# Moving 183 tasks of an ordered five-engine program to other places in their engine's order

## The chip, the cores and the metric

The kernel runs on one core of a Trainium2 chip. The core has five engines with an instruction queue each: TensorE (PE in the profile), ScalarE (ACT), VectorE (DVE), GpSimd (POOL) and SyncE (SP, which here only issues transfers), and 16 DMA engines that move the data. The metric is the device time of one execution in microseconds (us). Before the change it is 190.21 us, the median of three runs (189.45 to 190.45).

## The reference

A gated linear attention is followed by a feed-forward block. Only the order of operations matters here:

```python
f = 1.0 / (1.0 + np.exp(-f_logit))               # B, H, S, D = 4, 8, 768, 48
for t in range(S):
    state = f[:, :, t, :, None] * state + np.einsum('bhd,bhe->bhde', k[:, :, t], v[:, :, t])
    y[:, :, t] = np.einsum('bhd,bhde->bhe', q[:, :, t], state)
x = y.transpose(0, 2, 1, 3).reshape(B * S, H * D)   # 3072 x 384
h = x @ w_in                                     # 384 x 2048
g = h * (1.0 / (1.0 + np.exp(-h)))
out = g @ w_out                                  # 2048 x 384
```

## The kernel before

The sequence of 768 steps is cut into 6 chunks of 128, and there are 4 batches: 24 units, numbered u = 0 to 23, four units of one chunk after the other. Two neighbouring units form a pair P. Each unit is a chain of small tasks, and each task belongs to one engine. In the names below the number is the unit (or its pair's first unit), and for the feed-forward tasks a second number is the piece.

- SP: `f`, `k`, `q`, `v` load a unit (192 KB each) or, from unit 4 on, a pair (384 KB each), all at L485. `wi_0..3` (L505) and `wo_0..3` (L510) load the weights, 768 KB each. `qkD` and `xD` transpose by DMA for later units (L592, L625), `so` (L562) stores a unit's output; units up to 10 are stored from POOL, the others from SP.
- ACT: `E`, `L` (L492, L494) make the logarithm of the gate; `ia`, `a`, `al` (L572, L574, L576) are exponentials of its running sum; `s1` and `si` (L526, L536) are the SiLU of a feed-forward piece. SiLU and the exponentials need different function tables, so a table load (L680) stands wherever the order goes from one kind to the other. `co_2` is a weight cast.
- PE: `cs` (L565, L569) the running sum; `tq` (L588) a transpose of q and k; `sc` (L599) the scores; `y` (L608, L612) the chunk's output; `yT` (L620) its transpose; `d` (L630) the state's increment; `m1` (L529, one unit) and `mi` (L540, a pair) the first feed-forward product in pieces; `mo` (L551) the second one, four tasks a unit.
- DVE: `qg` (L582), `qkc` (L590), `at` (L603), `yc` (L616), `xc` (L622), `sd` (L635, L637), the output copies `oa` and `oc` (L554, L559), and the casts `ci_3`, `co_1`.
- POOL: `ki` (L578), `vb` (L580), `su` (L641, the new state), the early stores, and the casts `ci_0`, `ci_1`, `ci_2`, `co_0`, `co_3` (L520).

The chain of one unit is `f, E, L, cs, ia, a`; then `qg` (needs `a` and `q`) and `ki` (needs `ia` and `k`); then `tq` and `qkc` (or `qkD`), `sc`, `at`, `y`, `yc`, `yT` and `xc` (or `xD`). Then `m1`/`mi` of piece j (needs the x of its units and the weight cast `ci`), `s1`/`si`, `mo`, `oc`, `so`.

The order is decided while the program is built, not on the chip. `make_tasks` (L81) lists the tasks with dependencies, buffers and priorities. `schedule` (L208) plays them through an estimate, first free, which yields one fixed order per engine, and then once more with that order; this second pass hands out the buffer numbers. `planned` (L376) joins the two. `idle` (L386) finds stretches in which PE is expected to wait, and fills them with multiplications of a block of zeros (`warm`, L650, matmuls at L653). Then each task is emitted, and each engine works off its tasks strictly in this order.

Many buffers are few: one PSUM bank each for `cs`, `tq`, `sc` and `yd` (used by `y` and `d`), three for the feed-forward products (`mlp`), two staging buffers `wt` for the four `wo` pieces, three output buffers `o`. So a task also waits until the earlier user of its buffer has been read. For instance `cs_5` needs the only `cs` bank, which `qg_4` still reads; and `wo_2` needs the staging buffer that `co_0` empties.

```python
    schedule(tasks, slots, cfg, cfg["margin"])
    fixed = {e: sorted([t for t in tasks if t.eng == e], key=lambda t: (t.start, t.idx)) for e in ENGINES}
    schedule(tasks, slots, cfg, 0.0, fixed=fixed)
```

Of the kernel before, what the change touches and what calls it, by code (L numbers as in the profile page):

```python
# [24 lines left out]
    margin=0.35,  # L25
# [11 lines left out]
    first=0,  # L37
# [25 lines left out]
ROW = {2: 0.097, 4: 0.178, 6: 0.235}  # L63
CAST_ENGINES = ('DVE', 'ACT', 'POOL')
CAST = dict(DVE=0.9, ACT=1.3, POOL=1.6)
DMA = dict(f=LOAD, k=LOAD, q=LOAD, v=LOAD, qkD=TURN, xD=TURN, wi=WEIGHT, wo=WEIGHT, so=STORE)


class Task:
    def __init__(self, name, eng, dur, prio, deps=(), acq=(), use=(), mode=None, phase=None, load=0.0):  # L70
        self.name, self.eng, self.dur, self.prio = name, eng, dur, prio
        self.deps, self.acq, self.use = list(deps), list(acq), list(use)
        self.mode, self.phase, self.load = mode, phase, load

# [6 lines left out]
def make_tasks(cfg):  # L81
# [4 lines left out]
    def add(name, *a, **k):  # L86
        t = Task(name, *a, **k)
        T[name] = t
        tasks.append(t)
        return t  # L90
# [78 lines left out]
    for j in range(4):  # L169
        for m, (x, w, N) in enumerate((("wi", "ws", NI), ("wo", "wt", NO))):  # L170
            e = cfg["cast"][4 * m + j]
            add(("ci" if x == "wi" else "co", j), e, CAST[e], cfg["rank0"]["cw"] + 1.0 * j + 4.0 * m, deps=[T[x, j * N // 4]], use=[I[w, j * N // 4]])

# [31 lines left out]
    return tasks, T  # L205


def schedule(tasks, slots, cfg, margin=0.0, fixed=None, dur=None):  # L208

    for i, t in enumerate(tasks):  # L210
        t.idx, t.start, t.end, t.succ, t.ready, t.left = i, None, None, [], 0.0, len(t.deps)
# [17 lines left out]
    q = {"hw": [], "sw": []}  # L229
    events, pend = [0.0], []  # L230
    events.append(busy["SP"])
    now, dma_t, done, EPS = 0.0, 0.0, 0, 1e-7

    def finish(t, when):
        nonlocal done
        t.end = when
        done += 1
        lat = LAT[t.eng] if not t.load else 0.06
        for s in t.succ:
            l = (0.15 if s.eng == "ACT" else 0.0) if s.eng == t.eng and not t.load else lat  # L240
            if s.eng == "PE" and t.eng != "PE":
                l += margin
            s.ready = max(s.ready, when + l)
            s.left -= 1
            if not s.left:
                waiting[s.eng].append(s)
            heapq.heappush(events, s.ready)
        for x in dict.fromkeys([*t.acq, *t.use]):
            x.users -= 1
            if not x.users:  # L250
                free[x.cls].append((when + lat, x.slot))
                heapq.heappush(events, when + lat)

    def heads():
        h = q["hw"][0] if q["hw"] and q["hw"][0][2] <= dma_t + EPS else None
        s = q["sw"][0] if q["sw"] and q["sw"][0][2] <= dma_t + EPS else None
        if h and s:
            rate = (h[4] / (h[4] + s[4]), s[4] / (h[4] + s[4]) * 1.04)
        else:
            rate = (1.0, 1.0)  # L260
        nxt = [x[0][2] for x in q.values() if x and x[0][2] > dma_t + EPS]
        if h:
            nxt.append(dma_t + h[1] / rate[0])
            over = sum(x[1] for x in q["hw"]) - DEPTH
            if over > EPS:
                nxt.append(dma_t + over / rate[0] + EPS)
        if s:
            nxt.append(dma_t + s[1] / rate[1])
        return h, s, rate, min(nxt) if nxt else None

    def dma_to(upto):
        nonlocal dma_t
        while dma_t < upto - EPS:
            h, s, rate, nxt = heads()
            step = min(upto, nxt if nxt is not None else upto) - dma_t
            dma_t += step
            for k, v, r in (("hw", h, rate[0]), ("sw", s, rate[1])):
                if v:
                    v[1] -= r * step
                    if v[1] <= EPS:  # L280
                        q[k].pop(0)
                        if q[k] and q[k][0][4] != v[4] and k == "hw" and TURN[2] in (q[k][0][4], v[4]):
                            q[k][0][1] += cfg["turn_cost"]
                        heapq.heappush(pend, (dma_t + v[3], v[0].idx))
                        heapq.heappush(events, dma_t + v[3])

    def can(t):
        need = {}
        for x in t.acq:
            if x.slot is None:  # L290
                need[x.cls] = need.get(x.cls, 0) + 1
        return all(sum(f <= now + EPS for f, _ in free[c]) >= n for c, n in need.items())

    def pick(e, cand):
        key = lambda t: (t.prio, t.idx)
        if e != "ACT":
            return min(cand, key=key)
        best = {m: min((t for t in cand if t.mode == m), key=key, default=None) for m in ("exp", "silu")}
        free_one = min((t for t in cand if t.mode is None), key=key, default=None)
        mine, other = best[st["mode"]], best["silu" if st["mode"] == "exp" else "exp"]  # L300
        if free_one and (mine is None or free_one.prio < mine.prio):
            return free_one
        if other is None:
            return mine
        if mine is None:
            oldest = min(max(t.ready, st["last"]) for t in cand)
            hold = cfg["hold_" + st["mode"]]
            if now + EPS >= oldest + hold:
                return other
            heapq.heappush(events, oldest + hold)  # L310
            return None
        return other if other.prio < mine.prio - cfg["keep_" + st["mode"]] else mine

    n = 0
    while done < len(tasks):
        n += 1
        if n > 100000:
            raise RuntimeError("no end")
        while events and events[0] <= now + EPS:
            heapq.heappop(events)  # L320
        dma_to(now)
        while pend and pend[0][0] <= now + EPS:
            when, i = heapq.heappop(pend)
            finish(tasks[i], when)
        moved = True
        while moved:
            moved = False
            for e in engines:
                if busy[e] > now + EPS or (e == "SP" and sum(x[1] for x in q["hw"]) > DEPTH + 2 * EPS):
                    continue  # L330
                if fixed is not None:
                    if at[e] == len(fixed[e]):
                        continue
                    t = fixed[e][at[e]]
                    if t.left or t.ready > now + EPS or not can(t):
                        continue
                    at[e] += 1
                else:
                    cand = [t for t in waiting[e] if t.ready <= now + EPS and can(t)]
                    t = pick(e, cand) if cand else None  # L340
                    if t is None:
                        continue
                    waiting[e].remove(t)
                moved = True
                begin = now
                if t.mode is not None and t.mode != st["mode"]:
                    st["mode"] = t.mode
                    begin = max(begin, st["last"] + TABLE)
                for x in t.acq:
                    if x.slot is None:  # L350
                        got = min(fs for fs in free[x.cls] if fs[0] <= now + EPS)
                        free[x.cls].remove(got)
                        x.slot = got[1]
                t.start = begin
                busy[e] = begin + D(t)
                if e == "ACT":
                    st["last"] = busy[e]
                heapq.heappush(events, busy[e])
                if t.load:
                    sp = e == "SP"  # L360
                    first, land, packet = DMA[t.name[0]]
                    q["hw" if sp else "sw"].append([t, t.load, now + first, land, packet])
                else:
                    heapq.heappush(pend, (busy[e], t.idx))
        nxt = heads()[3]
        nxt = [x for x in (events[0] if events else None, pend[0][0] if pend else None, nxt) if x is not None]
        if not nxt:
            raise RuntimeError(f"stuck at {now:.2f}: {[t.name for t in tasks if t.end is None][:12]}")
        now = max(min(nxt), now + 1e-5)
# [6 lines left out]
def planned(cfg, slots):  # L376

    tasks, T = make_tasks(cfg)
    schedule(tasks, slots, cfg, cfg["margin"])
    fixed = {e: sorted([t for t in tasks if t.eng == e], key=lambda t: (t.start, t.idx)) for e in ENGINES}  # L380
    schedule(tasks, slots, cfg, 0.0, fixed=fixed)
    order = sorted(tasks, key=lambda t: (t.start, t.idx))
    return order, idle(order, slots, cfg)

# [326 lines left out]
```

## Time and profile before

| quantity | value |
|---|---|
| time, median of 3 runs | 190.21 us (189.45 to 190.45) |
| the profiled execution's own time | 188.87 us |
| its span, first to last instruction | 187.1 us |
| PE busy | 174.3 us (93% of the span) |
| ACT busy | 131.1 us (70%) |
| DVE busy | 95.8 us (51%) |
| POOL busy | 70.6 us (38%) |
| read from and written to HBM | 25.17 MB, 4.72 MB |
| granted PE clock | 1.00 |

The profile comes from one execution; its own time is 1.77 us longer than its span. Busy time of PE contains the filling matmuls on zeros (10.6 us) and the overlap of pipelined matmuls, so that it is not a measure of useful work. For that the start times of neighbouring tasks on PE are of more use: the distance from one task's first matmul to the next one's. An entry such as `atm L603 <- PE sc L599` in the waits means that the DVE instruction at L603, which writes `atm`, waited for the matmuls at L599. In the chain of work an entry of SPq is the time in which SP issues a transfer, and an entry of DMA is a transfer in flight.

### The profile page before, as it was taken

The page shows a single profiled execution, that of the slowest core. Times are in us where ns is not written, and L with a number is a line of the kernel's source. Part 1 is how long each engine was busy: PE and PEld are TensorE (multiplying, and loading weights), DVE is VectorE, ACT ScalarE, POOL GpSimd, SP SyncE. Part 2 cuts the span into 40 slices and gives each one's busy share as a digit, 9 for nine tenths or more (in the row PEclk, how much of TensorE's full clock was granted, in tenths as well). Part 3 has the DMA queues.
Part 4 walks back from the last instruction along what each step waited for, and adds up shares of the span by engine and source line. Part 5 has one row for each costly group of instructions (what it writes and reads, how often), then busy time and mean ns, then how long its engine had stood idle before and what let it go on. Part 6 is the DMA issues. An engine that isn't in the chain of part 4 may idle for free.

```text
span 187.1 us, 4715 instructions
## 1 busy us (share of the span) xinstructions
PE 174.3 (93%) x1925; PEld 134.0 (72%) x1925; DVE 95.8 (51%) x185; ACT 131.1 (70%) x217; POOL 70.6 (38%) x112
## 2 busy tenths in 40 slices
PE   5987768989999999979999999999999999999991
PEld 2454758667878879768787786678688886966960
DVE  4269436425877773565527736875542415261011
ACT  4442845988797898998988788668669996810810
POOL 2337647345727470561752742490352006000000
PEclk9999999999999999999999999999999999999999
DMA  6999999999989999999597589588996566413101
GB/s 125 217 216 333 381 351 303 277 191 251 244 193 224 223 246 237 217 226 217 126 185 169 129 177 179 101 118 209 186 151 169 129 121 135 103 21 105 46 17 67
DMA packets 120389, 34.22 MB, mean 183 GB/s; under 512 B 116128, under 2 KB 117792, under 8 KB 120368
## 3 DMA queue, kind: packets, MB, share of 16 engines
q1 hardware_dynamic: 119664, 31.76, 78.3%
q0 software_dynamic: 704, 2.16, 3.2%
q8 instruction: 15, 0.25, 0.5%
q14 instruction: 6, 0.05, 0.1%
HBM read 25.17 MB, written 4.72 MB: 160 GB/s over the span
## 4 chain that ended last, share of the span: by engine, by line
PE 70%; SPq 11%; DMA 8%; ACT 5%; issue 2%; POOL 1%; DVE 1%; DVEq 0%; ACTq 0%
PE mlp L551 29%; PE mlp L540 24%; DMA q<-in_q_dram 8%; SPq L485 7%; PE mlp L529 4%; PE sc L599 3%; SPq L505 3%; PE yd L612 2%; PE yd L608 2%; PE cs L565 2%; ACT L680 2%; PE tq L588 1%; PE yd L630 1%; SPq L510 1%; ACT hT L536 1%
## 5 line engine op out<-in xcount | busy, mean ns | idle before, releaser
L551 PE MATMUL mlp<-w_out,hT 128*128 128x384 bf16 x384 | 69.9, 326 | 0.0
L536 ACT ACTIVATE hT<-mlp 128x512 bf16<-128x512 f32 x72 | 41.7, 597 | 17.4 <-PE mlp L540 14.9
L540 PE MATMUL mlp<-xT,w_in 128*128 128x256 bf16 x432 | 51.5, 273 | 1.1 <-ACT hT L536 1.0
L551 PEld LDWEIGHTS <-hT 128*128 128x128 bf16 x384 | 34.8, 97 | 19.5
L540 PEld LDWEIGHTS <-w_in 128*128 128x128 bf16 x432 | 46.3, 114 | 3.2 <-issue 1.3
L578 POOL TENSOR_TENSOR qk<-k,ia 128x384 bf16<-128x384 f32 x24 | 24.0, 1000 | 53.2 <-ACT al L576 33.2
L603 DVE TENSOR_TENSOR atm<-sc,triu 128x512 bf16<-128x512 f32 x48 | 30.9, 685 | 19.6 <-PE sc L599 19.6
L680 ACT ACT_TABLE_LOAD x23 | 29.5, 1283 | 0.4
L641 POOL TENSOR_TENSOR st<-sd,al 48x192 bf16<-48x192 f32 x40 | 21.0, 524 | 15.8 <-DVE sd L635 8.6
L572 ACT ACTIVATE ia<-cs 128x384 f32<-128x384 f32 x24 | 11.8, 490 | 15.4 <-PE cs L569 10.4
L616 DVE CAST yb<-yd 128x384 bf16<-128x384 f32 x24 | 13.3, 554 | 15.9 <-PE yd L612 15.8
L559 DVE COPY o<-mlp 128x384 f32<-128x384 f32 x22 | 12.2, 556 | 17.8 <-PE mlp L551 14.1
L529 PE MATMUL mlp<-xT,w_in 128*128 128x128 bf16 x288 | 18.7, 220 | 1.9 <-DVE w_in L520 1.6
L582 DVE TENSOR_TENSOR qk<-q,cs 128x384 bf16<-128x384 f32 x24 | 13.2, 550 | 13.4 <-ACT cs L574 8.4
L529 PEld LDWEIGHTS <-w_in 128*128 128x128 bf16 x288 | 16.9, 114 | 2.7 <-DVE w_in L520 1.8
L526 ACT ACTIVATE hT<-mlp 128x512 bf16<-128x512 f32 x24 | 13.6, 597 | 6.8 <-PE mlp L529 6.4
L580 POOL CAST vb<-v 128x384 bf16<-128x384 f32 x24 | 11.6, 505 | 8.9 <-DMA v<-in_v_dram 8.8
L492 ACT ACTIVATE e<-f 128x768 f32<-128x768 f32 (+1 forms) x14 | 10.5, 747 | 5.9 <-DMA f<-in_f_logit_dram 5.9
L635 DVE TENSOR_TENSOR sd<-yd,st 128x384 f32<-128x384 f32 x16 | 8.9, 555 | 8.3 <-PE yd L630 6.2
L574 ACT ACTIVATE cs<-cs 128x384 f32<-128x384 f32 x24 | 11.4, 477 | 0.6
L653 PE MATMUL mlp<-blank 128*128 128x512 bf16 (+3 forms) x32 | 10.6, 466 | 1.0 <-DVE blank L660 1.0
L494 ACT ACTIVATE lf<-e 128x768 bf16<-128x768 f32 (+1 forms) x14 | 10.5, 750 | 0.3
(43 smaller groups left out, 143.9 us busy)
## 6 DMA issues: line engine op xcount, KB each, us to landing
f<-in_f_logit_dram SPq DMA_DIRECT2D x10, 384.0 KB, 5.7
k<-in_k_dram SPq DMA_DIRECT2D x10, 384.0 KB, 5.9
q<-in_q_dram SPq DMA_DIRECT2D x10, 384.0 KB, 5.9
v<-in_v_dram SPq DMA_DIRECT2D x10, 384.0 KB, 5.6
ws<-in_moe_w_in_dram SPq DMA_DIRECT2D x4, 768.0 KB, 9.0
wt<-in_moe_w_out_dram SPq DMA_DIRECT2D x4, 768.0 KB, 8.0
out_dram<-o SPq DMA_DIRECT2D x13, 192.0 KB, 2.1
out_dram<-o POOLq DMA_DIRECT2D x11, 192.0 KB, 3.9
```

What stands on the lines that cost most here:

```text
L485: nc.sync.dma_start(out=dst, in_=SRC[x].rearrange("b h s d -> s (b h) d")[c * C:(c + 1) * C, b * H:(b + n) * H])
L526: return nc.scalar.activation(at("hT", P)[:, 4 * j:4 * j + 4, i * C:(i + 1) * C], h, AF.Silu)
L529: nc.tensor.matmul(h[:, r, :], w_tile(kk, 4 * j + r), at("xT", P)[:, kk, i * C:(i + 1) * C], start=(kk == 0), stop=(kk == KT - 1))
L536: return nc.scalar.activation(at("hT", P)[:, 2 * j:2 * j + 2, :], h, AF.Silu)
L540: nc.tensor.matmul(h[:, i, :], w_tile(kk, n), at("xT", P)[:, kk, :], start=(kk == 0), stop=(kk == KT - 1))
L551: nc.tensor.matmul(o, at("hT", P)[:, n, i * C:(i + 1) * C], w_rows(n), start=(n % (NT // 2 if half else NT) == 0), stop=(n == NT - 1 or ha ...
L578: nc.gpsimd.tensor_mul(at("qk", u)[:, 1, :, 0:D], at("k", P)[:, i], at("ia", u))
L582: nc.vector.tensor_mul(at("qk", u)[:, 0, :, 0:D], at("q", P)[:, i], at("cs", u)[:, 0:HD].rearrange("p (h d) -> p h d", d=D))
L603: nc.vector.tensor_mul(at("atm", u)[:, r], at("sc", u)[:, r], triu[:, None, :].to_broadcast([C, NP, C]))
L616: nc.vector.tensor_copy(at("yb", u), at("y", u))
L641: nc.gpsimd.tensor_mul(at("st", u)[lo:lo + D, :, r * D:(r + 1) * D], at("sd", u)[lo:lo + D, :, r * D:(r + 1) * D], at("al", u)[lo:lo + D, ...
L680: nc.scalar.preload_act_table_set(SETS[after[t.idx]])
```

## The change

The fixed orders are made as before. Then 183 named tasks are taken out of their engine's list (63 of PE, 36 of ACT, 35 of POOL, 26 of DVE, 23 of SP), and each is put back right behind another named task of the same engine. The second pass runs with these lists. It also uses longer estimates for the weight transfers and casts, and counts every landing 0.3 later. That pass fixes three things: the order across engines in which tasks are emitted, which buffer number each task gets, and where and how many zero matmuls fill PE (158 units of 128 columns instead of 112). No task is added or removed.

```diff
 CAST = dict(DVE=0.9, ACT=1.3, POOL=1.6)
+SECOND, LATE, CAST_DUR = dict(wi=2.09, wo=1.95), 0.3, dict(DVE=1.12, ACT=1.3, POOL=1.47)
 DMA = dict(f=LOAD, k=LOAD, q=LOAD, v=LOAD, qkD=TURN, xD=TURN, wi=WEIGHT, wo=WEIGHT, so=STORE)
+MOVED = (
+    ("cs_1", "y_0"), ("tq_1", "d_0"), ("sc_1", "tq_1"), ("yT_1", "sc_2"), ("m1_0_1", "m1_1_1"),
+    ("m1_0_2", "m1_1_2"), ("m1_0_3", "yT_2"), ("m1_1_0", "m1_2_1"), ("sc_3", "m1_2_0"), ("m1_2_2", "m1_2_3"),
...
+    ("yT_8", "y_9"), ("cs_10", "yT_8"), ("mo_6_1", "d_8"), ("mi_4_1", "mi_4_2"), ("mi_4_0", "sc_10"),
+    ("tq_11", "cs_12"), ("d_9", "tq_11"), ("mi_4_4", "mi_4_5"), ("mi_4_3", "mi_4_4"), ("sc_11", "mi_4_6"),
...
+    ("yT_12", "cs_15"), ("yT_13", "cs_16"),
+    ("mi_6_0", "mi_6_1"), ("cs_17", "mi_6_2"), ("mi_6_3", "mi_6_4"), ("mi_6_5", "mi_6_6"), ("y_14", "mo_11_0"),
...
+    ("sc_22", "mi_10_2"), ("mo_21_0", "mo_20_1"), ("mo_21_3", "mi_11_0"), ("al_0", "E_1"), ("E_2", "al_0"),
+    ("L_2", "L_1"), ("al_1", "a_1"), ("E_3", "al_1"), ("al_2", "a_2"), ("ia_3", "al_3"), ("s1_1_3", "s1_2_1"),
...
+    ("si_3_1", "si_3_2"), ("si_3_0", "si_3_1"), ("E_14", "E_12"), ("si_4_5", "si_4_2"), ("L_14", "E_16"),
...
+    ("ci_3", "xc_2"), ("qg_3", "sd_2"), ("xc_3", "yc_3"), ("oa_0", "xc_3"), ("sd_4", "qg_6"), ("qg_7", "xc_5"),
...
+    ("oc_12", "sd_15"), ("xc_14", "qg_19"), ("qg_20", "yc_18"), ("sd_17", "qg_21"), ("oc_14", "sd_17"),
+    ("sd_18", "oc_15"), ("sd_19", "oc_16"), ("ci_1", "ki_1"), ("vb_2", "ci_2"), ("su_0", "ki_3"), ("co_3", "vb_3"),
+    ("su_2", "co_3"), ("so_2", "vb_5"), ("su_3", "so_2"), ("so_3", "ki_6"), ("vb_7", "ki_7"), ("su_4", "vb_7"),
...
+    ("su_6", "ki_10"), ("so_5", "su_8"), ("so_4", "ki_11"), ("so_6", "so_4"), ("su_9", "vb_14"), ("ki_12", "so_7"),
+    ("vb_13", "ki_13"), ("vb_15", "su_10"), ("ki_14", "vb_15"), ("su_11", "vb_17"), ("so_8", "su_11"),
+    ("ki_16", "su_13"), ("su_12", "ki_16"), ("vb_18", "su_14"), ("su_15", "su_16"), ("vb_20", "ki_21"),
+    ("vb_21", "su_17"), ("su_19", "ki_22"), ("vb_23", "ki_23"), ("f_2", "v_0"), ("wi_1", "q_1"), ("f_3", "k_2"),
+    ("v_3", "f_4"), ("wo_3", "v_3"), ("k_6", "q_6"), ("v_6", "f_8"), ("q_8", "v_8"), ("f_10", "v_10"),
+    ("k_10", "f_10"), ("f_12", "v_12"), ("q_16", "f_14"), ("k_14", "q_14"), ("q_12", "f_16"), ("v_14", "q_12"),
...
+)
@@
+        self.label = "_".join(str(x[0] if isinstance(x, tuple) else x) for x in name)
@@
-                    q["hw" if sp else "sw"].append([t, t.load, now + first, land, packet])
+                    q["hw" if sp else "sw"].append([t, t.load, now + first, land + late, packet])
@@
-    schedule(tasks, slots, cfg, 0.0, fixed=fixed)
+    by = {t.label: t for t in tasks}
+    for name, _ in MOVED:
+        fixed[by[name].eng].remove(by[name])
+    for name, after in MOVED:
+        line = fixed[by[name].eng]
+        line.insert(line.index(by[after]) + 1 if after else 0, by[name])
+    for t in tasks:
+        t.load = SECOND.get(t.name[0], t.load)
+        t.dur = CAST_DUR[t.eng] if t.name[0] in ("ci", "co") else t.dur
+    schedule(tasks, slots, cfg, 0.0, fixed=fixed, late=LATE)
```

The orders that result, where the prediction speaks of them (before, then after):

```
SP   before  f_0 k_0 q_0 v_0 f_1 k_1 q_1 v_1 f_2 k_2 q_2 v_2 wi_1 f_3 wi_2 wo_1 wi_3 k_3 wi_0 q_3 wo_0 wo_3 v_3 f_4 wo_2 k_4 q_4
SP   after   f_0 k_0 q_0 v_0 f_2 f_1 k_1 q_1 wi_1 v_1 k_2 f_3 q_2 v_2 wi_2 wo_1 wi_3 k_3 wi_0 q_3 wo_0 f_4 v_3 wo_3 wo_2 k_4 q_4
POOL before  ki_0 vb_0 ki_1 vb_1 su_0 ki_2 vb_2 ci_1 ci_2 su_1 ki_3 ci_0 su_2 co_0 co_3 vb_3 su_3 ki_4
POOL after   ki_0 vb_0 ki_1 ci_1 vb_1 ki_2 ci_2 vb_2 su_1 ki_3 su_0 ci_0 co_0 vb_3 co_3 su_2 ki_4
PE   before  m1_1_3 d_2 m1_2_1 tq_3 m1_0_0 m1_1_0 sc_3 m1_2_0 m1_2_2 m1_2_3 mo_0_0 mo_0_1 y_3 mo_1_0 mo_1_1 d_3 yT_3 mo_2_0 mo_2_1 cs_4 m1_3_0 m1_3_1 mo_2_2 mo_2_3 cs_5 tq_4
PE   after   m1_1_3 d_2 m1_2_1 m1_1_0 tq_3 m1_0_0 m1_2_0 sc_3 m1_2_3 m1_2_2 mo_0_0 y_3 mo_0_1 yT_3 mo_1_0 d_3 mo_1_1 mo_2_0 cs_4 mo_2_1 m1_3_0 m1_3_1 mo_2_2 mo_2_3 cs_5 tq_4
ACT  both    s1_2_0 s1_2_2 s1_2_3 E_4 L_4 co_2 ia_4 al_4 a_4
ACT  before  si_3_7 ia_10 al_10 a_10 E_12 L_12 ia_11 al_11 a_11 E_14 si_4_0
ACT  after   si_3_7 ia_10 al_10 a_10 E_12 E_14 L_12 ia_11 al_11 a_11 si_4_0
```

## The prediction, made before the run

> **What bounds the kernel now.** I first read the head of the page and its slices of time (tenths busy, 4.7 us each).
>
> ```profile
> span 187.1 us, 4715 instructions
> PE 174.3 (93%) x1925; PEld 134.0 (72%) x1925; DVE 95.8 (51%) x185; ACT 131.1 (70%) x217; POOL 70.6 (38%) x112
> ...
> PE   5987768989999999979999999999999999999991
> ...
> DMA  6999999999989999999597589588996566413101
> ```
>
> PE is full after some 30 us; before that it has holes, and the DMA engines are full instead. Then the waits of PE alone:
>
> ```profile
> PE cs L565 <- ACT lf L494: 2.2, 2, 1.1
> PE mlp L529 <- DVE w_in L520: 1.6, 1, 1.6
> PE mlp L540 <- ACT hT L536: 1.0, 1, 1.0
> ...
> PE tq L588 <- DVE qk L582: 0.8, 1, 0.8
> PE cs L565 <- DVE qk L582: 0.8, 1, 0.8
> ```
>
> That is little, but fillers hide waits. So I gathered the instruction list by task and took start-to-start distances on PE. They hardly scatter: `m1` 0.67, `mi` 0.655, `mo` 0.65, `tq` 0.44, `sc` 0.33, `y` 0.37 (0.20 in the first chunk), `d` and `yT` 0.17, `cs` 0.265 (0.16 in the last chunk). Times their counts these make 158.9 us. `cs_0` starts at 4.56 and the last task ends at 183.1, so 19.6 us are lost between tasks: 14.5 before `tq_3` starts at 28.77, 0.92 at `cs_5` (41.31), 1.14 at `mi_4_3` (82.48), 0.23 at `mi_6_3` (109.26), and some 0.1 ahead of each `sc`. The work is not changed; the losses are all there is to win, and from 28.8 on about 2.3 us of them are waits.
>
> What holds the two larger ones? The chain of work, by start and length, ahead of `cs_5`:
>
> ```profile
> 30.42 1.48 POOL w_out L520
> 31.89 0.02 issue
> 31.91 0.53 SPq L510
> 32.44 0.04 issue
> 32.48 0.43 SPq L485
> 32.92 0.04 issue
> 32.96 7.62 DMA q<-in_q_dram
> ```
>
> SP stands still from 27.20 until POOL's `co_0` has emptied the staging buffer that `wo_2` needs; behind `wo_2` come `k_4` and `q_4`. `q_4` lands at 40.58, `qg_4` ends at 41.26 and frees the `cs` bank. At 82 us it is ACT (start, length):
>
> ```profile
> 74.85 1.28 ACT L680 ACT_TABLE_LOAD   x1
> 76.15 0.49 ACT L572 ACTIVATE ia<-cs 128x384 f32<-128x384 f32 x1
> ...
> 79.70 0.84 ACT L492 ACTIVATE e<-f 128x768 f32<-128x768 f32 x1
> 80.54 1.28 ACT L680 ACT_TABLE_LOAD   x1
> ```
>
> Two table loads and 4.38 us of exponentials lie between `si_3_7` and `si_4_0`, and only three `mlp` banks cover them.
>
> **What the skill says.** The Trainium skill, "PSUM — Partial Sum Buffer", section "Engine vs sequencer instructions", has ScalarE, VectorE and GpSimdE queues as strict FIFO and matmuls in program order; the trace agrees (SP, too, holds `k_4` for 4.7 us behind `wo_2`). "DMA: Bandwidth & Descriptors", "Specifications", asks for 512 B and more for line rate: here 192 B rows moved at about 0.22 MB per us and the weights' 2 KB and 6 KB rows at about 0.4. Its section "Issuing engines are not separate DMA queues" says that transfers share the same engines whoever issues them. So early stores on POOL compete with loads. "ScalarE: Activation LUTs", "What ACT_TABLE_LOAD costs", gives 1.28 us and a drain of 1.38 for each switch; the trace shows 1283 ns and an idle gap of 1.31 in all, no drain. I use 1.31.
>
> **The change part by part.**
>
> *Up to 28 us.* `wi_1` goes ahead of `v_1, k_2, q_2, v_2`, `f_2` ahead of `f_1`, `cs_1` behind `y_0`. By landing distances (single load 0.87, first weight 3.75, later weights 2.0) `wi_1` lands near 13.7 instead of 17.5, `f_3` near 16.1 instead of 18.25, `k_2` and `q_2` some 4 us later. `E_3` now stands before `ia_2` on ACT, so unit 2 starts late: `ia_2` 16.7 instead of 13.8. Yet `sc_2` comes at about 19.7 as before, and `m1` starts at 20.7 instead of 20.06. All this has cover: before, PE stood 1.85 us at `m1_0_3` for `ci_3`, whose weight lands at 24.40. `ci_3` now waits for `xc_2` too, about 0.2 later, but `yT_2` is done before it. Had `f_3` no more than a us of further delay, nothing follows.
>
> *The anchor at 28.* `wi_0`, `q_3` and `wo_0` have the same transfers ahead of them in both orders, on full DMA engines: 27.30, 28.07 and 29.95 as before. `ci_0` runs behind `su_0` (ends about 27.4) until 28.9, and `m1_1_0`, now ahead of `tq_3`, starts at 28.95. In tasks of the lengths above, PE reaches the point behind `sc_3` and the three `m1` 0.15 later than before.
>
> *To `cs_5`.* PE now does `m1_2_3` before `m1_2_2`, but ACT keeps `s1_2_2` before `s1_2_3`: `s1_2_3` ends at 34.5 instead of 33.84, then table 1.31, `E_4`, `L_4` end at 37.5 (36.87). PE comes to `cs_4` at 37.0: a new wait of 0.55. From there 3.6 us of tasks lead to `cs_5` at 41.1. The other limit: `su_2` leaves the way of `co_0`, which runs from the landing of `wo_0`, 29.95, to 31.45 instead of 31.89; `wo_2` and `q_4` come 0.4 earlier, 40.2, and `cs_5` could start at 40.9. The later limit holds: 41.1, **0.2 won**.
>
> *41 to 67.* Swaps of `m1`/`mo` pieces, `E_6` before `a_5` (`tq_5` 0.25 later, inside its slack), `cs_9` 3 us later (its reader `ia_9` waits for a table load anyway), late stores `so_0, so_1, so_4`. I compared each place with the end of its producers and bank: no PE task loses more than 0.05. **0.**
>
> *67 to 84.* `cs_10` and `yT_8` go behind `mi_3_7` (0.435 together): `mi_3_7`, `si_3_7` and the table load come 0.46 earlier. ACT then does the same 4.38 us; it ends on `a_11`, so that one step is a little longer, 4.5. `si_4_0` ends at 82.1, and PE resumes at 82.15 with the same tasks done: **0.35 won**. Cover needed: `f_14` must land before 77.5; it moves from 76.92 to about 75.1.
>
> *Afterwards.* `ki_12` waits behind `so_7` (2.5 later), `ki_16` behind `so_8, so_9, so_10, su_13` (2.7 later); `qkD_12` and `qkD_16`, with `v_18` and `f_20` behind them on SP, follow. `sc_12` had 3.74 and `sc_16` 3.55 of slack, `E_20` 2.92: just covered, and lost one for one beyond that. At `mi_6_3` the pieces follow ACT's order: 0.15 of 0.23 won. `oc_14` behind `sd_17` makes `mi_8_1` 0.05 late. The end (copy, store, 4 us) stays.
>
> *Fillers* add 46 units, 56 ns each when warm, 2.6 us, in waits for `ci_3`, `ci_0` and the first units: nothing while those waits last.
>
> Sum: 0.2 + 0.35 + 0.15 - 0.05 = 0.65 us. The profiled execution of 188.87 becomes 188.2; the median of 190.21, which is 1.34 above it, becomes **189.55**.
>
> **Rivals.**
>
> *Early weight, early gain.* The first weight piece took 3.75 us between landings, the later ones 2.1: a start loss of 1.65. If small loads around `wi_1` fill it, `wi_0`, `ci_0`, `wo_0` and `q_4` all come about 1.6 earlier, and PE keeps it through `cs_5`: 190.21 - 0.65 - 1.6 = 188.0. For it: DMA moved less than usual at 13 to 15 us. Against: `f_3` was queued there already and did not fill it.
>
> *The start loss paid twice* (the slower side). After `wi_1` come five small loads, then `wi_2`. If a weight behind small loads always starts so slowly, `wi_0` lands at 28.95, and `ci_0`, PE and `cs_5` are 1.65 late: 190.21 - 0.65 + 1.65 = 191.2. It decides from 0.65 on, and makes 0.5% from 1.6. For it: `wi_1` itself. Against: `wi_0` and `wo_0`, each behind one small load, took 2.1 and 1.9.
>
> *Nothing.* New waits like the one at `cs_4` may eat all: 190.2. Half of the moves change the order of pieces that are never late.
>
> **How the numbers follow.** Chances: forecast 45% (189.0 to 190.1), early gain 25% (187.4 to 188.7), paid twice 22% (190.7 to 191.8), nothing 8%. 0.5%, 0.95 us, is about what a measurement of this kernel can tell from no change, so the border is 189.26 and 191.16. The forecast lies at it: a third of it, all of the early gain: 0.40 faster. Two thirds of the paid-twice case and a remainder of unseen stalls: 0.20 slower. The rest, 0.40, within. The range leaves out the outer parts of both rivals: 187.9 to 191.4.
>
> **What would show it.** SP's issue of `wo_2` near 31.5; `wi_0` landing near 27.3 (26 or 29 for the rivals); a wait of `cs_4` for `L_4` of about half a us near 37; `cs_5` near 41.1; the PE wait for `hT` near 82 at 0.6 instead of 1.0; no wait at `sc_12`, `sc_16`. A wait of PE over 0.3 us anywhere after 84 us, or a landing of `wi_0` more than 0.7 from 27.3, makes the prediction wrong.

## The result and the profile after

The changed kernel is slower: 190.9 us, the median of 22 runs, beside 189.88 us, the median of 22 runs of the kernel before. The ratio is 1.0053, with a 95% interval from 1.0031 to 1.0074, so about 1.0 us (0.6 to 1.4) was lost where 0.65 was to be won. Ratios and their intervals, here and below, leave out the few executions over 1.5% slower than the fastest of their kernel, and are worked out from all the others, not from the two medians printed beside them. The three runs known before had their median at 190.21; the 22 have it 0.33 lower. The profiled execution of the changed kernel took 191.54 us, 0.6 more than its median, and the one of before, 188.87, is below its own; the pair of profiles therefore shows a larger difference (2.7 us of span) than the medians, and single times read from it below carry some of that scatter.

The head of the page and its slices, after the change:

```profile
span 189.8 us, 4733 instructions
...
PE 177.3 (93%) x1938; PEld 134.2 (71%) x1938; DVE 95.8 (50%) x185; ACT 129.4 (68%) x217; POOL 70.3 (37%) x112
...
PE   5988778998999999999999999998999999999991
...
DMA  6998999999998999989979549969898805611201
```

The span is 2.7 us longer. PE is 3.0 us busier; the zero matmuls account for it, as their busy time rose from 10.6 to 13.8 (46 more units, some 70 ns each by this, where the prediction had 56). The waits of PE (sum, count, longest):

```profile
PE yd L663 <- POOL vb L631: 1.6, 1, 1.6
PE cs L616 <- ACT lf L545: 1.5, 2, 1.3
...
PE sc L650 <- DMA qkT<-qk: 0.7, 1, 0.7
PE mlp L580 <- POOL w_in L571: 0.6, 1, 0.6
PE cs L616 <- DVE qk L633: 0.5, 1, 0.5
...
PE mlp L591 <- ACT hT L587: 0.2, 1, 0.2
```

The lines of the changed kernel are 51 higher (L540 is now L591). Two things are as the prediction wanted them: the wait for `hT` at 82 us fell from 1.0 to 0.2, and `cs` waits less for `qk`. Three are new. At 24 us `y_2` waits for `vb_2`, which on POOL now stands behind the weight cast `ci_2` (the wait of `m1_0_3` for `ci_3`, next in PE's order, fell from 1.6 to 0.3). PE waits for the weight cast `ci_0` (`w_in`), and in the second half for a transposed `qkT`. The chain of work shows where the head went (start, length):

```profile
32.22 1.48 POOL w_out L571
...
33.72 0.34 SPq L561
...
34.11 0.42 SPq L536
...
34.59 8.83 DMA q<-in_q_dram
```

`co_0` follows the landing of its weight at once, as foreseen, but that landing is at 32.17, not 29.95; `q_4` lands at 43.41 instead of 40.58, and `cs_5` starts at 44.14 instead of 41.31.

Worked out once more by start-to-start distances on PE, the balance of the two profiles is: first task 0.34 later (as was the landing of `f_0`, whose place is the same, so this is scatter), 2.5 more lost up to `cs_5`, 0.1 less from there to 73 us, 0.75 less at `mi_4`, 0.23 less at `mi_6_3`, 0.72 more at `sc_18`, 0.17 more at `mi_9_3`. That is 2.6; the last task starts 2.7 later. So the question is what happened ahead of 44 us, and only then what happened at `sc_18`.

### The profile page after: what moved, and what is told of

It is laid out like the page before. It is cut to its first block, busy times and chain, and to the rows that moved or that the text cites. A ratio compares the mean times of both kernels' runs of the same rounds, so it can differ in the third digit from the quotient of the medians.

```text
span 189.8 us, 4733 instructions
## 1 busy us (share of the span) xinstructions
PE 177.3 (93%) x1938; PEld 134.2 (71%) x1938; DVE 95.8 (50%) x185; ACT 129.4 (68%) x217; POOL 70.3 (37%) x112
## 4 chain that ended last, share of the span: by engine, by line
PE 67%; SPq 12%; DMA 12%; ACT 3%; issue 2%; POOL 1%; DVE 1%; DVEq 0%; POOLq 0%
PE mlp L602 28%; PE mlp L591 23%; SPq L536 8%; DMA q<-in_q_dram 5%; DMA wt<-in_moe_w_out_dram 4%; SPq L556 4%; PE mlp L580 4%; PE sc L650 3%; DMA qkT<-qk 3%; PE yd L663 2%; PE yd L659 2%; PE tq L639 1%; PE cs L616 1%; PE yd L681 1%; PE tq L671 1%
## 5 line engine op out<-in xcount | busy, mean ns | idle before, releaser
L602 PE MATMUL mlp<-w_out,hT 128*128 128x384 bf16 x384 | 71.1, 326 | 0.0
L587 ACT ACTIVATE hT<-mlp 128x512 bf16<-128x512 f32 x72 | 41.1, 597 | 19.8 <-PE mlp L591 17.8
L591 PE MATMUL mlp<-xT,w_in 128*128 128x256 bf16 x432 | 51.7, 273 | 0.2 <-ACT hT L587 0.2
L591 PEld LDWEIGHTS <-w_in 128*128 128x128 bf16 x432 | 46.2, 114 | 2.4 <-issue 0.5
L577 ACT ACTIVATE hT<-mlp 128x512 bf16<-128x512 f32 x24 | 13.6, 596 | 9.9 <-PE mlp L580 9.5
L704 PE MATMUL mlp<-blank 128*128 128x512 bf16 (+3 forms) x45 | 13.8, 430 | 1.3 <-DVE blank L711 1.0
L641 DVE COPY qkT<-tq 128x1024 bf16<-128x1024 bf16 x12 | 8.3, 690 | 7.1 <-PE tq L639 7.1
L663 PE MATMUL yd<-vb,atm 128*128 128x48 bf16 x192 | 9.0, 183 | 2.3 <-POOL vb L631 1.6
```

Of the source, the lines that this page charges most:

```text
L577: return nc.scalar.activation(at("hT", P)[:, 4 * j:4 * j + 4, i * C:(i + 1) * C], h, AF.Silu)
L587: return nc.scalar.activation(at("hT", P)[:, 2 * j:2 * j + 2, :], h, AF.Silu)
L591: nc.tensor.matmul(h[:, i, :], w_tile(kk, n), at("xT", P)[:, kk, :], start=(kk == 0), stop=(kk == KT - 1))
L602: nc.tensor.matmul(o, at("hT", P)[:, n, i * C:(i + 1) * C], w_rows(n), start=(n % (NT // 2 if half else NT) == 0), stop=(n == NT - 1 or ha ...
L704: nc.tensor.matmul(buf["mlp", bank][:, 0:w * C].rearrange("p (n c) -> p n c", c=C), blank, blank[:, None, :].to_broadcast([C, w, C]), star ...
```

## The experiments

Theory A: SP's new order in the head is the loss, and the later moves are a gain. Its rivals: the moves of the other engines in the head (C), or the new estimates with their other buffer numbers and fillers (D). Each run is compared with the kernel before on the same chip; the kernels' lines are 54 higher than before. A short diff stands for each, against the changed kernel.

**The head alone.** 39 of the 183 moves, those of tasks that run before about 41 us: five of SP, five of POOL, six of DVE, nine of ACT, 14 of PE.

```diff
+HEAD = ("f_2", "wi_1", "f_3", "v_3", "wo_3", "ci_1", "vb_2", "su_0", "co_3", "su_2", "qg_1", "qkc_1", "ci_3", "qg_3", "xc_3",
+        "oa_0", "al_0", "E_2", "L_2", "al_1", "E_3", "al_2", "ia_3", "s1_1_3", "s1_0_0", "cs_1", "tq_1", "sc_1", "yT_1", "m1_0_1",
+        "m1_0_2", "m1_0_3", "m1_1_0", "sc_3", "m1_2_2", "mo_0_1", "yT_3", "mo_1_1", "mo_2_1")
+MOVED = tuple(m for m in MOVED if m[0] in HEAD)
```

> Only the 39 moves of tasks that run before cs_5 (about the first 42 us): 5 of SP, 5 of POOL, 6 of DVE, 9 of ACT, 14 of PE; the other 144 tasks keep their places; new estimates as in the change. Theory A (SP's order: wi_1 between small loads keeps SP from issuing, and wi_0, wo_0, q_4 land about 2 us late): the whole loss sits here, wi_0 lands near 29.4 and cs_5 starts near 43.5 to 44, the time is 1.5 to 2.3 us (0.8 to 1.2%) above before. Theory B (the loss is in the later moves, such as the wait at sc_18): within 0.5 us of before.

Measured: 190.85 beside 189.44 us, ratio 1.0071 (1.0053 to 1.0090). The loss is 1.35 us (1.0 to 1.7), a little below the 1.5 to 2.3 that A expected. `wi_0` landed at 28.77, `q_4` at 42.92, `cs_5` started at 43.65.

**The other 144 moves alone.**

```diff
+MOVED = tuple(m for m in MOVED if m[0] not in HEAD)
```

> Only the 144 moves of tasks that run after cs_5, the first 42 us in the order of before; new estimates as in the change. Theory A: wi_0 lands near 27.3, cs_5 near 41.3, the wait at mi_4 shrinks by 0.75 and that at mi_6 by 0.2 as in the profile of the changed kernel, so 0.8 to 1.0 us (0.4 to 0.5%) below before, or about 0.2 below if the wait at sc_18 (0.8) comes with them. Theory B: 0.5 to 1.5 us above before.

Measured: 188.97 beside 189.44 us, ratio 0.9966 (0.9946 to 0.9985). The head is as before (`wi_0` 27.43, `cs_5` 41.58). PE's waits after 60 us, all of them:

```profile
PE sc L653 <- DMA qkT<-qk: 0.7, 1, 0.7
PE mlp L594 <- ACT hT L590: 0.2, 1, 0.2
```

The gain at `mi_4` and the loss at `sc_18` both belong to this half. The gain of 0.64 lies between the two figures that A named (0.8 to 1.0, or 0.2 with the wait at `sc_18`). The halves, +1.35 and -0.64, add up to +0.7, which the interval of the whole holds.

**Three moves of SP alone.**

```diff
+MOVED = tuple(m for m in MOVED if m[0] in ("f_2", "wi_1", "f_3"))
```

> Only three moves of SP: f_2 behind v_0, wi_1 behind q_1, f_3 behind k_2. Every other task keeps its place. Theory A: SP needs about 4 us to issue the load behind v_1 and k_2, the DMA engines run short near 14 us, wi_0 lands near 29.4, cs_5 near 43.3 or later, the time is 1.5 to 2.3 us above before. Theory C (the moves of PE, ACT, POOL in the head are the cause, the loads alone are harmless): wi_0 within 0.5 of 27.3 and the time within 0.5 us of before.

Measured: 190.67 beside 189.44 us, ratio 1.0045 (1.0017 to 1.0073), a loss of 0.85 us (0.3 to 1.4), less than A's 1.5 to 2.3; `wi_0` 28.71, `q_4` 43.50, `cs_5` 44.23.

**No move at all**, only the new estimates and so the new buffer numbers and fillers (163 units). Of the casts, only those on VectorE have a longer estimate than before (1.12 instead of 0.9); on POOL it is shorter (1.47 instead of 1.6).

```diff
+MOVED = ()
```

> No task is moved; only the new estimates are in force, so that buffer numbers, the emission order and the fillers (163 units instead of 112) come from the second pass. Theory A: within 0.3 us of before, as all added fillers lie in waits for weights. Theory D (fillers and buffer numbers cost): 0.5 to 2 us above before, with fillers right ahead of late PE tasks.

Measured: 189.37 beside 189.44 us, ratio 0.9988 (0.9967 to 1.0009); `wi_0` 27.68, `cs_5` 41.72. D falls: no loss is seen. C isn't needed for most of the loss, since three moves of SP make 0.85 us of it without any other engine's; whether the other engines' moves in the head add to it (1.35 against 0.85, with intervals that overlap) is not shown.

**One move of SP alone.**

```diff
+MOVED = (("wi_1", "q_1"),)
```

> Only one move: wi_1 behind q_1, with f_2 and f_3 where they were. Theory A (the place of wi_1 alone makes the loss): wi_0 lands at 28.5 to 29.4, cs_5 2 us or more later than in the kernel before, and the time is 0.8 to 1.5 above it. Rival (f_2 ahead of f_1 and f_3 ahead of q_2 are needed for it: f_3 is the load that is stuck at issue for 3 to 4 us): wi_0 lands below 28, and the time is within 0.4 of the kernel before.

Measured: 189.98 beside 189.5 us, ratio 1.0045 (1.0023 to 1.0066); `wi_0` 28.66, `q_4` 41.76, `cs_5` 42.49. The first piece of weight in its early place makes the same ratio as the three moves, 0.85 us (0.4 to 1.25), at the lower end of what A expected; `cs_5` came 1.2 later, not 2.

### What the early weight does

The issues of SP in the changed kernel (start, length), from the load of `v_1` on:

```profile
8.87 0.49 SPq L536 DMA_DIRECT2D v<-in_v_dram  x1
9.40 0.62 SPq L536 DMA_DIRECT2D k<-in_k_dram  x1
10.07 4.15 SPq L536 DMA_DIRECT2D f<-in_f_logit_dram  x1
14.27 0.70 SPq L536 DMA_DIRECT2D q<-in_q_dram  x1
15.02 0.70 SPq L536 DMA_DIRECT2D v<-in_v_dram  x1
15.76 0.94 SPq L556 DMA_DIRECT2D ws<-in_moe_w_in_dram  x1
```

The issue of `f_3` lasts 4.15 us and ends at 14.22, just ahead of the landing of `wi_1` at 14.40. The Trainium skill, "Perfetto Trace Analysis", section "DMA Instruction — HWDGE (DVE, Sync)", says that such a record begins when the waits for semaphores are over and lasts until all descriptors are generated, and that the DMA engines may start earlier when more are generated than fit in the descriptor buffer. The trace fits that reading: in the kernel before the first twelve small loads cost SP 0.5 to 1.1 us each to issue, and here this one 4.15. `q_2`, `v_2` and `wi_2` are issued only after it. What the DMA engines do meanwhile, from 8 to 28 us in 40 slices of half a us (tenths busy, then GB/s), is this in the kernel before:

```profile
DMA  9999999999879999999999999999999999999999
GB/s 251 229 208 247 205 212 206 230 248 157 162 274 332 317 284 249 293 359 381 367 393 397 389 406 418 393 422 362 335 336 347 319 372 333 337 297 366 336 418 369
DMA packets 10638, 6.28 MB, mean 314 GB/s; under 512 B 8864, under 2 KB 8864, under 8 KB 10637
```

and this in the changed kernel:

```profile
DMA  9999569999996279899979999999999999999999
GB/s 195 220 234 219 65 213 336 348 332 303 278 245 139 54 148 242 142 176 231 230 184 280 286 336 356 381 410 422 389 385 414 393 351 327 333 348 357 364 325 325
DMA packets 10788, 5.66 MB, mean 283 GB/s; under 512 B 9137, under 2 KB 9137, under 8 KB 10787
```

Before, there is one dip, at 13 us, where the first piece of weight follows small loads. After, there are three: at 10 us, the same start of `wi_1`; at 14.0 to 15.5, where the engines stand at 6, 2 and 7 tenths, because nearly all rows of `wi_1`, `v_1` and `k_2` have been moved by then and SP refills one small load at a time; and around 18, where `wi_2` starts behind small loads. In the same 20 us 0.62 MB less is moved, which at the 0.314 MB per us of before are 2.0 us, and `wi_0` lands 2.06 later. The pair overstates the shift: `wi_0` landed at 27.30 to 28.23 in six profiles with the old order of loads (27.6 on average), and at 28.71, 28.77 and 29.36 in the three with this one (28.9), which is 1.3 later. SP's being held (J in the texts below) and a slow start of pieces of weight behind small loads (K) are both in this profile. In distances between landings, place by place in the queue, after against before: the eight loads ahead of `wi_1` 0.59 more, `wi_1` 0.12, the three small loads behind it 0.28 less, `q_2` 0.27 more, `v_2` 0.80, `wi_2` 0.54; together 2.04. The first of these lies ahead of the landing of any weight, and is at least in part scatter: `v_0`, which has the same place in both orders, was 0.74 later already.

**Two pieces of weight in the early place.**

```diff
+MOVED = (("wi_1", "q_1"), ("wi_2", "wi_1"))
```

> Only two moves: wi_1 behind q_1 as in the change, and wi_2 directly behind wi_1, so that two pieces of weight stand in the queue when SP comes to the small loads. Theory J (SP gets stuck behind its own queue, DMA runs dry meanwhile, and the slow start comes from that): the two pieces keep DMA busy while SP is stuck, wi_2 follows wi_1 at the usual 2.1, and wi_0 lands at 27.3 to 27.9, as in the kernel before; time within 0.5 of it. Rival K (a piece of weight behind small loads alone always starts slowly, whatever the queue does; it is paid once more at wi_3, behind four small loads): wi_0 lands near 29, ci_0, q_4 and cs_5 follow, and the time is 1 us or more above the kernel before.

Measured: 190.13 beside 189.5 us, ratio 1.0028 (1.0009 to 1.0047); `wi_0` 27.96, `q_4` 42.23, `cs_5` 42.96. `wi_2` landed 2.06 behind `wi_1`, as J expected, while SP was held at `f_2` and `k_2` for 3.4 and 3.1 us. But `wo_1`, next behind six small loads, landed 3.22 after the load ahead of it: the slow start was paid again, on another piece. `wo_0` too came late, 3.13 behind `q_3`, where the other runs have 1.9 to 2.0; why is open. The result lies between the two expectations.

**The early piece issued by ScalarE.** SP has the small loads only.

```diff
-            return nc.sync.dma_start(out=at("ws", rest[0]), in_=w_in_src[:, :, n:n + w])
+            return (nc.scalar if rest[0] == 1 else nc.sync).dma_start(out=at("ws", rest[0]), in_=w_in_src[:, :, n:n + w])
```

with the one move of `wi_1`.

> As the run with wi_1 alone behind q_1, but wi_1 is issued by ScalarE, near 7 us, not by SP; the loads on SP keep their order. Theory L (the small loads behind wi_1 hold SP at issue for some 3.5 us, so the next piece of weight is issued too late[...]): SP is not held between 7 and 14 us, wi_2 is issued at 11 to 12.5 instead of 14.8, lands by 20.4, wi_0 lands at 27.6 or earlier, and the time is within 0.5 us of the kernel before or below it. Rival K (a piece of weight behind small loads alone starts slowly whenever it is issued, and now two pieces stand behind such loads): wi_2 again lands 3 us or more after the load ahead of it, wi_0 lands at 28.4 or later, and the time is 0.8 us or more above the kernel before.

Measured: 190.66 beside 189.5 us, ratio 1.0061 (1.0037 to 1.0086); `wi_0` 29.04. SP's issues in this run:

```profile
7.19 0.71 SPq L539 DMA_DIRECT2D f<-in_f_logit_dram  x1
7.94 4.16 SPq L539 DMA_DIRECT2D k<-in_k_dram  x1
12.15 0.70 SPq L539 DMA_DIRECT2D q<-in_q_dram  x1
```

SP is held for 4.16 us all the same, until 12.10, and `wi_1` lands at 12.11. So the weight needn't stand in SP's own queue to hold SP: the small loads get no further while it is moved. Even `q_1`, issued at 5.3 and landing at 9.1 in the kernel before, landed at 12.39 here. Theory L, that another issuing engine would free SP, falls. `wi_2` landed 3.48 after the load ahead of it, as K said.

**Never more than two small loads between two pieces.**

```diff
+MOVED = (("wi_1", "q_1"), ("wi_2", "f_2"), ("wo_1", "q_2"))
```

> Only SP's order in the head: q_1, wi_1, v_1, f_2, wi_2, k_2, q_2, wo_1, v_2, f_3, wi_3, k_3, wi_0, so that never more than two small loads stand between two pieces of weight. Theory J (a weight starts slowly because the DMA engines have run dry or are refilled by SP one small load at a time; here a piece of weight always stands in the queue while SP is held): only wi_1 starts slowly, wi_2, wo_1 and wi_3 each land 3.2 to 3.7 after the piece before them (2 small loads of 0.75 and 2.0), wi_0 lands at 27.3 to 27.9 as in the kernel before; time within 0.6 us of it. Rival K (the slow start is paid by every piece that follows small loads, two of them are enough): the pieces land 4.5 or more apart, wi_0 lands at 29 or later, and the time is 1 us or more above the kernel before.

Measured: 191.4 beside 190.25 us, ratio 1.0070 (1.0048 to 1.0091); `wi_0` 28.30. `wi_2`, `wo_1`, `wi_3` landed 4.22, 4.88 and 4.00 after the piece before them, of which 2.61, 3.41 and 2.75 behind the last small load; a piece behind another piece takes 1.9 to 2.2. The same view of the DMA engines as above:

```profile
DMA  9989999999699999995799899994798999999999
GB/s 219 151 263 361 352 393 286 260 265 226 225 324 287 383 307 268 258 285 112 246 332 381 355 270 257 252 93 64 229 365 287 381 317 277 291 377 414 381 288 337
```

No stretch as at 14 us of the changed kernel is left, in which only small loads refill the engines, but dips stand where `wo_1` and `wi_3` follow small loads (at 17 and 21 us, down to 112 and 64 GB/s). SP was through with the issue of `wo_1` at 15.97, a us ahead of its dip; with that of `wi_3` only at 20.71, so there lateness isn't excluded. The first six rows of `wi_3`, at 21.4, took 0.8 to 1.0 us each in the trace, against 0.09 later on. J alone is too little. But K isn't borne out in full: it expected pieces 4.5 or more apart, which only `wo_1` was, and `wi_0` (28.30) is short of its 29. The time is 1.3 us above before, in K's range, but that is no clean test of K, as this order also delays small loads: `k_2` and `q_2` land at 17.05 and 17.64 instead of 11.69 and 12.73, and PE stood 3.5 us at `cs_3`.

One caution: with an unchanged order of loads, `wi_0` landed at 27.30, 27.43, 27.41, 27.68, 27.70 and 28.23 in six profiled executions, and `cs_5` started anywhere from 41.31 to 42.66. The profile of before, with which this document compares, has the earliest of both. So 28.0 to 28.3 in a single profile, or a `cs_5` later by a us, tells little; the ratios decide.

### What the later moves do

**Without the move of `xD_16`.** In the changed kernel SP transposes the output of unit 16 (`xD_16`) ahead of q and k of unit 18 (`qkD_18`). SP in the changed kernel:

```profile
119.71 1.52 SPq L643 DMA_TRANSPOSE qkT<-qk  x1
121.28 2.55 SPq L676 DMA_TRANSPOSE xT<-yb  x2
124.00 4.39 SPq L643 DMA_TRANSPOSE qkT<-qk  x2
```

and in the kernel before:

```profile
117.91 1.25 SPq L592 DMA_TRANSPOSE qkT<-qk  x1
119.20 1.25 SPq L625 DMA_TRANSPOSE xT<-yb  x1
120.62 4.77 SPq L592 DMA_TRANSPOSE qkT<-qk  x2
```

Counted from the start of `sc_17`, `qkD_18` is issued 2.04 ahead instead of 3.62, and then flies 5.14 instead of 3.32; PE waits. The longer flight isn't an effect of the move: 3.32 is the shortest of all profiles, and in eight others, in which `qkD_18` was issued 3.6 ahead as before, the flight was 4.22 to 5.42 and nothing more than before was lost. What the move took is the lead.

```diff
+MOVED = tuple(m for m in MOVED if m[0] not in HEAD and m[0] != "xD_16")
```

> The 144 later moves without the one of xD_16 (and of nothing in the head). Theory A (what the later moves lose is the wait of sc_18 for the transposed qk, caused by xD_16 standing ahead of qkD_18 on SP): xD_16 goes back behind qkD_18, the wait of 0.86 at sc_18 is gone, and the time falls by about 0.8 below that of the later moves, to 1.1 to 1.5 below the kernel before (ratio about 0.993). Rival (the transposition of qk would be late anyway, because stores and loads moved past it fill the queue): sc_18 still waits 0.4 or more, and the time stays at 0.3 to 0.7 below the kernel before.

Measured: 188.53 beside 189.5 us, ratio 0.9947 (0.9924 to 0.9970), that is 1.0 below (0.6 to 1.4), a little less than the 1.1 to 1.5 expected. The loss at `sc_18`, 0.86 in the run with the 144 later moves, fell to 0.46 only: `qkD_18` was issued 3.15 ahead of `sc_17`, but now flew 5.88. So putting `xD_16` back took away about half of it; the rest came with a long flight, as the rival had it, although the time is better than the rival's 0.3 to 0.7.

**The best of it.** Also without the move of `mi_8_7`, and on POOL `su_2` behind `co_3`, so that `co_0` follows `ci_0` at once.

```diff
+MOVED = tuple(m for m in MOVED if m[0] not in HEAD and m[0] not in ("xD_16", "mi_8_7")) + (("co_3", "vb_3"), ("su_2", "co_3"))
```

> As the one before it, also without the moves of mi_8_7, and with one pair of my own: on POOL co_3 goes behind vb_3 and su_2 behind co_3, so that co_0 follows ci_0 at once (the part of the whole change that my forecast priced at 0.4 for q_4 and cs_5). Theory: mi_9_3 no longer waits (0.17 won), q_4 lands 0.4 earlier than in the kernel before (near 40.4), cs_5 starts 0.4 to 0.7 earlier, 41.0 or so, and the time is 1.5 to 1.9 below the kernel before (ratio about 0.991). Rival (the 0.4 is taken again by SP or by DMA, which is full there): q_4 and cs_5 as in the run before this, and the time within 0.3 of it.

Measured: 188.25 beside 189.5 us, ratio 0.9935 (0.9913 to 0.9957), 1.2 us (0.8 to 1.65) faster than before and so better than both kernels, but less than the 1.5 to 1.9 expected. PE's waits after 60 us, all of them:

```profile
PE mlp L594 <- ACT hT L590: 0.2, 1, 0.2
```

`mi_9_3` no longer waits, and at `sc_18` 0.25 is lost. Whether `co_0` at once brought anything can't be told: `wo_2` was issued at 31.66 instead of 31.91, landed at 36.82 instead of 36.47, and `q_4` landed at 40.65, as before (40.58). But counted from the landing of `wo_0`, the issue of `wo_2` came 0.4 sooner than in the five other profiles with the old loads (1.55 against 1.94 to 1.96), while `q_4` landed 10.53 later, against 10.63 to 11.30 there, and 10.96 later in the next run, which has the same order on POOL. Single executions scatter more than the 0.4 at stake.

**The best with the early weight**, issued by ScalarE as above.

```diff
+MOVED = tuple(m for m in MOVED if m[0] not in HEAD and m[0] not in ("xD_16", "mi_8_7")) + (("co_3", "vb_3"), ("su_2", "co_3"), ("wi_1", "q_1"))
```

> The best version so far (later moves without those of xD_16 and mi_8_7, su_2 behind co_3), and wi_1 behind q_1, issued by ScalarE. Theory L: the early piece costs nothing, and DMA is full in the whole head, so that wi_0 lands 0 to 1.5 us earlier than in the best version (26 to 27.4), q_4 and cs_5 follow, and the time is 0 to 1.3 below that of the best version. Rival K: wi_0 lands 1 us or more later than in the best version, and so does the end.

Measured: 189.39 beside 189.5 us, ratio 0.9982 (0.9953 to 1.0011). The early weight costs 0.47% here (0.9982 against 0.9935), some 0.9 us (0.2 to 1.6, an estimate from the two intervals, which were measured on different chips). With that move alone it cost 0.45% issued by SP and 0.61% issued by ScalarE. `wi_0` landed at 28.12, 0.7 later than without it, less than the 1 us of rival K. L, which expected no cost, falls again.

**The step at `mi_4` alone**, with the two moves of DVE that this order of PE needs.

```diff
+MOVED = (("yT_8", "y_9"), ("cs_10", "yT_8"), ("yc_8", "qkc_9"), ("xc_8", "yc_9"))
```

> Only the step at 67 to 84 us: yT_8 and cs_10 behind y_9 and so behind mi_3_7 on PE, and yc_8, xc_8 on VectorE behind qkc_9 and yc_9, without which that order can't run. Theory (these two steps are what gives the gain at mi_4): the wait of PE at mi_4 falls from 1.14 of loss to 0.4 to 0.7, mi_6_3 keeps its 0.23, no wait at sc_18; time 0.4 to 0.75 us below the kernel before (ratio 0.996 to 0.998). Rival (the other later moves on PE and ScalarE are needed): the loss stays above 0.9, and the time within 0.2.

Measured: 189.63 beside 190.25 us, ratio 0.9971 (0.9953 to 0.9989), as the theory expected. The trace is less kind than the time: the loss at `mi_4_3` is 0.93 instead of 1.14, above the rival's bound of 0.9. The chain of work in this run shows why:

```profile
78.85 0.66 PE mlp L594 x6
79.50 0.16 PE cs L619
...
79.84 0.49 ACT ia L626
...
81.66 1.28 ACT L734
82.95 0.61 ACT hT L590
83.60 1.47 PE mlp L594 x12
```

Now PE itself is late: it does a piece at 78.85 ahead of `cs_11`, for which ACT then waits. The other later moves, some of which put such pieces behind, bring the rest: with all 144 of them the loss at `mi_4` is 0.39. By the trace the four moves give 0.2 of the 0.75; the measured 0.6 us (0.2 to 0.9) is more, and what the rest of it is stays open.

## Why the prediction was wrong

The forecast was 189.55, 0.65 below before; the result is 1.0 above before. The rival "the start loss paid twice" had put 191.2, also 1.0 above, and from like parts: 1.65 lost in the head and 0.65 won elsewhere, where the halves measured 1.35 and 0.64.

- **The step that failed is "the anchor at 28"**: the same transfers ahead on full DMA engines, hence the same landings of `wi_0`, `q_3` and `wo_0`. They came at 29.36, 30.13 and 32.17, each some 2.1 late (1.3 for `wi_0` over several profiles), and the move of `wi_1` alone cost 0.85 us. The sum of bytes ahead was the same, but not the pace. A piece of weight behind two or more small loads mostly took 0.5 to 1.8 us longer than behind another piece, `wo_1` of the run with pairs too, whose issue had ended a us ahead of its dip. And small loads issued behind a weight held SP until about the weight's landing (4.15 us at `f_3`), after which the engines ran nearly dry. The first of the two was in the profile of before, and the prediction named it as a rival; what it took as evidence against it, `wi_0` and `wo_0` at 2.1 and 1.9, came from pieces with one small load and a long queue ahead, and says nothing of five small loads. That SP could be held was visible too; these are its issues of `k_3` and `wi_0` before:

```profile
15.23 2.14 SPq L485
...
17.42 3.62 SPq L505
```

  There it cost nothing that can be seen, as `wi_0` landed 2.09 behind `k_3`, like other later pieces: long transfers stood in the queue. That the early place of `wi_1` causes the loss is shown; how the 2.06 divide between the two mechanisms is not settled, as no run has SP held without slow starts.
- **Up to 28 us** the first weight was put at 13.7 and landed at 14.40, `f_3` at 16.1 and 16.60. `sc_2` came 0.43 later than before, where no delay was expected. What was to cover such delays wasn't there: the weight of `ci_3` landed at 26.43, not 24.40, and `ci_3` started 0.39 behind it, for `xc_2`, where 0.2 was foreseen. So `m1_0_3` started at 27.82 instead of 25.44, and PE was 2.4 late before `ci_0`.
- **To `cs_5`**: the wait of `cs_4` for `L_4` came, 0.40 against 0.55. `co_0` did follow its weight at once, 0.4 sooner than before. But `q_4` landed 11.25 behind `wo_0`, not the 10.25 of the forecast (10.63 before). The prediction hadn't followed `wo_3`, which now stands behind `v_3` on SP:

```profile
26.94 4.90 SPq L536 DMA_DIRECT2D v<-in_v_dram  x1
31.95 2.10 SPq L561 DMA_DIRECT2D wt<-in_moe_w_out_dram  x2
```

  SP was held 4.90 at `v_3`, issued `wo_3` (with `wo_2` in the last line) at 31.95 instead of 24.52, and it landed at 37.43 (32.19 before), right ahead of `wo_2` (39.35) and `q_4`. In the best version, with `wo_3` in its old place, `q_4` came 10.53 behind `wo_0`; whether the forecast of 0.2 would hold with the old landings is open.
- **41 to 67**: 0 forecast; 0.1 less is lost there.
- **67 to 84**: right in its mechanism, its size was off: 0.75 won, not 0.35. Two terms were mis-sized. Measured from `cs_5`, ACT's last SiLU ahead of the table load started 0.56 earlier, not 0.46; and the stretch of ACT between its end and `si_4_0` took 6.85 us instead of the 6.99 of before, where the forecast had made it 0.12 longer. ACT after the change:

```profile
77.12 1.28 ACT L731 ACT_TABLE_LOAD   x1
...
79.39 1.57 ACT L543 ACTIVATE e<-f 128x768 f32<-128x768 f32 x2
80.86 0.83 ACT L545 ACTIVATE lf<-e 128x768 bf16<-128x768 f32 x1
...
82.66 1.28 ACT L731 ACT_TABLE_LOAD   x1
```

  `E_12` and `E_14` back to back take 1.57, not 2 times 0.84.
- **Afterwards**: `sc_12` and `sc_16` were just covered, as worked out, and `mi_6_3` lost nothing (0.23 won, 0.15 forecast). But the list of what SP issues was cut short: `ki_12` and `ki_16` with their transpositions were followed, `xD_16` moved ahead of `qkD_18` was not; `sc_18` lost 0.72 more than before, of which putting it back won about half; nor was `d_19` ahead of `mi_8_7`, 0.17 at `mi_9_3`. The text had named a wait of PE over 0.3 after 84 us as the sign of an error, and `sc_18` is one.
- **Fillers**: no cost is seen, as forecast; the run without moves is at 0.9988.
- The sum of gains outside the head, 0.35 and 0.15 less 0.05, was 0.45; the later moves alone measured 0.64 (0.3 to 1.0). That they are close is luck: more was won at `mi_4` than forecast, and 0.9 lost at `sc_18` and `mi_9_3`, where nothing was put. Nor does the trace show the 0.64: from `cs_5` to the last task of PE, the run with the later moves is 0.08 shorter than before; those without `xD_16`, the best and the one with four moves are 0.48, 0.86 and 0.22 shorter, each 0.3 to 0.6 less than its ratio says. What the surplus is stays open; the new estimates and fillers, which these runs share, may win a little ahead of `cs_5`, as the interval of the run without moves allows.

## What to carry to other kernels

Transfers ahead of a point can't be summed up by bytes when their rows differ: count how often the queue changes from small rows to large ones, and keep the pieces of weight together unless the trace shows a mix at full rate. A transfer moved forward can also hold whatever is issued behind it; ask what stands in the queue while the issuing engine is held, since in these traces long transfers covered it and short ones didn't. For every moved instruction, look at the next one of each kind that it passes on its queue, and not only at its own reader.

## What was not expected of the hardware

- Loads of 192 B rows issued behind one weight piece of 768 KB held the issuing engine at the second to fourth of them for 3.1 to 4.2 us, until within 0.2 us of the weight's landing in most runs (14.22 and 14.40; 12.38 and 12.55; 12.10 and 12.11), and also when another engine had issued the weight.
- Of the pieces of weight up to `wo_0`, one took 1.9 to 2.2 us between landings behind another piece; behind one small load mostly 1.9 to 2.5 (3.13 once); behind two 2.6 to 3.4; behind five or more mostly 2.6 to 4.0 (3.75 before, 3.87 after), but 2.08 once, for `wi_1` of the run with pairs.
- A transposition of q and k by DMA took between 3.3 and 5.9 us from issue to landing at the same place of the program (3.32, 4.57, 5.14, 5.88 in four of the runs). Issued 3.6 ahead of `sc_17`, even 5.42 was covered; issued 2.04 ahead, 5.14 was not.
